# Loading v of an attention unit in two transfers of 128 partitions, one per head

## The chip, the cores and the metric

The kernel runs on one core of a Trainium2 chip. The metric is the device time of one execution in microseconds. The kernel before took 674.45 us, the median of 3 runs (671.71 to 675.39).

A core has a matrix engine (TensorE, PE in the profile, with weight loads shown apart as PEld), three engines for elementwise work (VectorE or DVE, ScalarE or ACT, GpSimd or POOL), and SyncE (SP), which here only issues DMA transfers. Data lie in SBUF, 128 partitions wide; matrix products land in PSUM. Sixteen DMA engines move data between HBM and SBUF.

## The reference

Sparse attention over 8 batches, 8 heads, 576 positions and head dimension 64, then a feed-forward block on the 4608 x 512 result:

```
scores = scale * q @ k.T                   # per batch and head, 576 x 576
mask_local   = (rel >= 0) & (rel < 32)               # heads 0 to 3, rel = pos_i - pos_j
mask_strided = (rel >= 0) & (pos_j % 32 == pos_i % 32)   # heads 4 to 7
attn = softmax(where(mask, scores, -1e9));  out = attn @ v
x = out as (4608, 512)
h = maximum(maximum(x @ w1, x @ w2), x @ w3)         # 512 -> 768
result = h @ w_out                                   # 768 -> 512
```

All values are float32.

## The kernel before, in words

**Units.** Attention is cut into 32 units, four to a batch: two of strided heads, then two of local heads, each unit with two heads (`units`, L234). Units 0 and 1 are strided, 2 and 3 local, and so on. A unit goes through the steps S (scores, on TensorE), X (mask and maximum, DVE), E (exponentials, ACT), N (normalising and a transpose, DVE), V (the product with v, `values`, L426), H and L (the result split in a high and a low part, ACT and DVE).

**How v lies.** On the host, v is laid out in HBM per unit. A strided unit has 128 rows (32 of them used, and in batch 0 only 18), two heads, and 32 groups of 64 values. A local unit has 64 rows (a window of 64 keys), two heads and 18 blocks of 64 values. In SBUF, a unit's v is spread over the 128 partitions in four quarters j of 32 partitions: a quarter holds 8 groups (strided) or 5 blocks and the one before them (local). `load_v` (L256) loads it in one transfer for each quarter, both heads together: four for a strided unit (L280), of 128 KB, or 72 KB in batch 0; for a local unit three of 96 KB (L269), one of 48 KB for the shorter last quarter (L271), and one of 16 KB (L273) for the second half of the last window, which goes to partitions 96 to 127.

**Feed-forward.** The rows are worked in two parts. The first 1024 rows go through plain products (`ff_in`, L525, and `ff_out`, L555) with each float32 weight split into a high and a low part. The other 3584 rows go in four groups of 896 through seven products for each of nine pairs of weight blocks (L779), from weight sums that the kernel builds itself and keeps in HBM scratch; these are read back by a stream of 256 KB transfers (`load_next`, L668) with nine buffers, eight loaded ahead. Each group ends with the output product (L873). Units 16 to 31 run between the products of the first three groups.

**The opening.** The order of the first 100 us is written out by hand in two strings. `LOADS` orders the loads on SyncE: `q0` is one transfer of unit 0's q or k (288 KB; each unit has two), `v0` one of its v, `w0` a weight block of 512 KB. After it follow the remaining weight blocks (w14 to w17, then six of w_out). `OPENING` orders the steps: An to Dn and Cn convert weight block n (A: `convert_begin`, L164 on ACT, reads the loaded block; K: L173 on ACT; B: L183 and L186 on DVE; D: L196 and C: L205, L206 on ACT and POOL); Fn is the first feed-forward product of weight block n on TensorE (f and g are its halves), and Mn (`ff_max`, L540 to L546) takes its result out of one of the two PSUM banks that these products take turns with. Every engine works off its list in order.

```
A0 S0 X0 A1 K0 E0 B0 B1 A2 K1 ...
... f0 U4 D7 f1 K8 D8
C7 A9 L2 K9 S4 V3 X4 C8 H3 L3 g0 A10 g1 A11 A12 M0 B9 D9 K10 E4 B10 M1 D10 K11 B11 C9 D11 A13 F2 ...
```

So on ACT the step M0 stands behind A12, and on TensorE F2 follows g1.

**After the opening**, v and the q and k of a unit are loaded two units ahead: `values(n)` is followed by the loads of v of unit n + 2, and `scores(n)` by those of q and k. SyncE issues everything in one queue: all loads, the scratch writes and reads, and the output of the first part (L561). Each transfer signals one of eight semaphores, which go round, and waits until the transfer before on its semaphore has landed.

Of the kernel before, what the change touches and what calls it, by code (L numbers as in the profile page):

```python
# [7 lines left out]
F32 = mybir.dt.float32  # L8
# [7 lines left out]
B, H, S, D = 8, 8, 576, 64  # L16
STRIDE = 32
DM, DF, DO = 512, 768, 512
P = 128
# [6 lines left out]
NI = S // STRIDE  # L26
EARLY = B - 1
TQ, TK, NT = STRIDE, 2 * STRIDE, NI
# [3 lines left out]
MB = 5  # L32
MS = STRIDE // 4
PAIRED = 1
# [17 lines left out]


LOADS = """
q0 q0 w0 w1 w2 w3 q1 q1 w4 q2 q2 v0 w5 v0 v0 v0 q3 q3 w6 v1 v1 v1 w7 w8 v1 v2 w9 v2 v2 v2 w10 v2 q4 q4 v3 v3 w11 v3 v3 v3
v4 v4 w12 v4 v4 w13 q5 q5 v5 v5 v5 v5
"""
OPENING = """
A0 S0 X0 A1 K0 E0 B0 B1 A2 K1 K2 D0 D1 C0 N0 S1 A3 K3 C1 B2 B3 A4 X1 D2 D3 B4 S2 E1 C2 N1 A5 K4 D4 C3 V0
# [12 lines left out]
def fused_kernel(ctx, tc, qT, kT, qk_loc, qk_str, v_loc, v_str, m_loc, m_str, w1, w2, w3, w_out, out):  # L72
    nc = tc.nc
# [18 lines left out]
    io_early = early.enter_context(tc.tile_pool(name="io_early", bufs=1, side="right"))  # L92
# [7 lines left out]
    pin = tc.keep_in_program_order  # L100
# [17 lines left out]
    for sign in (1, -1):  # L118
        pin(nc.gpsimd.affine_select(
            out=unit, in_=unit, pattern=[[-sign, P]], base=0, channel_multiplier=sign, compare_op=ALU.is_ge, fill=0.0  # L120
# [18 lines left out]


    sources = [(w, j) for j in range(NJ) for w in range(3)] + [(None, j) for j in range(NJ)]
    raws, begun, weight = [], [], {}

    def load_weights(count):
        for _ in range(count):
            i, j = sources.pop(0)
            raw = (wo if i is None else wt).tile([P, 1024], I32, name=f"w{i}_{j}")
            if i is None:
                pin(nc.sync.dma_start(out=raw, in_=w_out.bitcast(I32)[j * P : (j + 1) * P, :]))
            else:  # L150
                src = (w1, w2, w3)[i].bitcast(I32)[:, j * 2 * P : (j + 1) * 2 * P]
                pin(nc.sync.dma_start(
                    out=raw.rearrange("p (c f) -> p c f", c=NKC), in_=src.rearrange("(c p) f -> p c f", p=P)
                ))
            raws.append((raw, i, j))

    def convert_begin():


        raw, i, j = raws.pop(0)  # L160
        words = raw.rearrange("p (n two) -> p n two", two=2)
        low, high = words[:, :, 0], words[:, :, 1]
        mag = wk.tile([P, 512], F32, name="work")
        pin(nc.scalar.activation(out=mag, in_=high.bitcast(F32), func=AF.Abs))  # L164
        pin(nc.gpsimd.tensor_scalar(out=mag, in0=mag, scalar1=W_MOST, scalar2=W_LEAST, op0=ALU.min, op1=ALU.max))
        lows.append(low)
        begun.append((low, high, mag, i, j))

    lows = []

    def convert_low():
        low = lows.pop(0)
# [62 lines left out]
    loaded, v_of = {}, {}  # L235
# [20 lines left out]
    def load_v(n):  # L256
        if n >= len(units):
            return
        b, p = units[n]
        if n in (2, 3):  # L260
            vt = io_early.tile([P, 2 * (MB + 1) * D], F32, name="v_t", bufs=2)
        else:
            vt = io.tile([P, 2 * MS * D], F32, name="v_t", bufs=2)
        if p < 2:

            v_of[n] = v = vt[:, : 2 * (MB + 1) * D].rearrange("p (h m d) -> p h m d", h=2, m=MB + 1)
            last = 3 * MB
            for j in range(3):
                pin(nc.sync.dma_start(out=v[32 * j : 32 * (j + 1)], in_=v_loc[b, p, :32, :, j * MB : (j + 1) * MB + 1, :]))  # L269
                yield  # L270
            pin(nc.sync.dma_start(out=v[96:, :, : NT - last, :], in_=v_loc[b, p, :32, :, last:, :]))  # L271
            yield
            pin(nc.sync.dma_start(out=v[96:, :, NT - last, :], in_=v_loc[b, p, 32:, :, NT - 1, :]))  # L273
            yield
        else:
            v_of[n] = v = vt.rearrange("p (h m d) -> p h m d", h=2, m=MS)
            for j in range(4):

                rows = NI if b < PAIRED else 32
                pin(nc.sync.dma_start(  # L280
                    out=v[32 * j : 32 * j + rows], in_=v_str[b, p - 2, :rows, :, j * MS : (j + 1) * MS, :]
                ))
                yield

    state = {}
# [124 lines left out]
    def pieces_of(b, p, step):  # L410

        at, end = b * S, (b + 1) * S
        while at < end:
            if at < CH:
                first, after, to = 0, CH, [x[:, p, :] for x in x_chunk(0)]
            elif at < PLAIN:
                first, after, to = CH, PLAIN, [place_of(-1)[:, p, :]]
            else:
                k = (at - PLAIN) // BL
                first = PLAIN + k * BL  # L420
                after, to = first + BL, [place_of(k)[:, p, :]]
            after = min(after, end)
            yield (at - b * S) // step, (after - b * S) // step, [x[:, at - first : after - first] for x in to]
            at = after

    def values(n):  # L426

        b, p = units[n]
        pt = state.pop(n)
        v = v_of.pop(n)  # L430
        loaded.pop(n)
        state[n] = to = []
        if p < 2:


            for m in (0, 2, 4, 1, 3, -1):
                for j in range(4):
                    last = min(MB, NT - j * MB) - 1
                    if m > last or (m < 0 and j == 0):
                        continue  # L440
                    js = slice(32 * j, 32 * (j + 1))
                    width = 64 if 0 <= m < last else 32
                    for h in range(2):
                        pin(nc.tensor.matmul(  # L444
                            o[h * D : (h + 1) * D, j, 32 * max(m, 0) : 32 * max(m, 0) + width],
                            v[js, h, m + 1, :],
                            pt[js, h, m * TK + 32 : m * TK + 32 + width] if m >= 0 else pt[js, h, :32],
                            start=m == 0,
                            stop=m == (-1 if j else 3),
                        ))  # L450
            for a0, a1, xs_to in pieces_of(b, p, 1):

                w, at = 32 * MB, a0
                while at < a1:
                    end = min(a1, (at // w + 1) * w)
                    j = at // w
                    if at % w == 0 and a1 >= at + w:
                        end = a1 // w * w
                        src = o[:, j : end // w, :w]
                    else:  # L460
                        src = o[:, j, at - j * w : end - j * w]
                    part = [x[:, at - a0 : end - a0] for x in xs_to]
                    if len(src.shape) == 3:
                        part = [x.rearrange("p (j q) -> p j q", q=w) for x in part]
                    to.append((src, *part))
                    at = end
            return
        if b >= PAIRED:
            for m in range(MS):
                for j in range(2):  # L470
                    js = slice(64 * j, 64 * (j + 1))
                    for h in range(2):
                        pin(nc.tensor.matmul(  # L473
                            o[h * D : (h + 1) * D, j, : 2 * MS * NI].rearrange("p (r m i) -> p r m i", r=2, m=MS)[:, :, m],
                            v[js, h, m, :],
                            pt[js, h, m * 64 : (m + 1) * 64].rearrange("p (r i) -> p r i", r=2)[:, :, :NI],
                            start=True,
                            stop=True,
                        ))
        for m in range(0 if b >= PAIRED else MS):  # L480
            for j in range(4):
                js = slice(32 * j, 32 * j + NI)
                for h in range(2):
                    pin(nc.tensor.matmul(
                        o[h * D : (h + 1) * D, j, m * NI : (m + 1) * NI],
                        v[js, h, m, :],
                        pt[js, h, m * 32 : m * 32 + NI],
                        start=True,
                        stop=True,
                    ))  # L490
        runs = 2 if b >= PAIRED else 4
        src = o[:, :runs, : 4 // runs * MS * NI].rearrange("p j (m i) -> p i j m", i=NI)
        for a0, a1, xs_to in pieces_of(b, p, STRIDE):
            to.append((src[:, a0:a1], *(x.rearrange("p (i j m) -> p i j m", i=a1 - a0, j=runs) for x in xs_to)))
# [144 lines left out]
    for step in OPENING.split():  # L639
        what, n = step[0], int(step[1:])  # L640
# [14 lines left out]
    def placed(n):  # L655

        values(n)
        list(load_v(n + 2))
        leading(n)
        rest(n)  # L660
# [311 lines left out]
```

## Time and profile before

| | |
|---|---|
| time, median of 3 runs | 674.45 us (671.71 to 675.39) |
| span of the profiled execution | 671.9 us (the page gives no other time of it) |
| TensorE clock granted, mean | 0.989 |
| TensorE busy | 647.1 us, 96% |
| DMA moved | 138.36 MB, mean 206 GB/s |
| v transfers | 64 strided (56 of 128 KB, 8 of 72 KB), 80 local (48 of 96 KB, 16 of 48 KB, 16 of 16 KB) |
| median from issue to landing | L280 (128 KB) 4.2 us, L269 3.3 us, L668 3.5 us |

A row of the waits reads: engine, line, `<-` what it waited for, then the sum in us, how many times, and the longest. A row of a timeline reads: start in us, length in us, engine, line, operation, output `<-` inputs, count, and in brackets the idle time before it and what ended it. Lines are those of the kernel before.

### The profile page before, as it was taken

The page shows a single profiled execution, that of the slowest core. Times are in us where ns is not written, and L with a number is a line of the kernel's source. Part 1 is how long each engine was busy: PE and PEld are TensorE (multiplying, and loading weights), DVE is VectorE, ACT ScalarE, POOL GpSimd, SP SyncE. Part 2 cuts the span into 40 slices and gives each one's busy share as a digit, 9 for nine tenths or more (in the row PEclk, how much of TensorE's full clock was granted, in tenths as well). Part 3 has the DMA queues.
Part 4 walks back from the last instruction along what each step waited for, and adds up shares of the span by engine and source line. Part 5 has one row for each costly group of instructions (what it writes and reads, how often), then busy time and mean ns, then how long its engine had stood idle before and what let it go on. Part 6 is the DMA issues. An engine that isn't in the chain of part 4 may idle for free.

```text
span 671.9 us, 18032 instructions
## 1 busy us (share of the span) xinstructions
PE 647.1 (96%) x7408; PEld 553.5 (82%) x7408; DVE 370.8 (55%) x515; ACT 336.5 (50%) x702; POOL 299.4 (45%) x291
## 2 busy tenths in 40 slices
PE   4689999999999999999999999999999999999997
PEld 3467877777778888888888888888899988999986
DVE  5886964676675666476345665643652563224240
ACT  4777656444264445446355455544444554444441
POOL 8779998599942233240134243004334401444410
PEclk9789999999999999999999999999999999999999
DMA  9999974567699777771377899228767714777411
GB/s 297 265 246 366 296 248 133 178 189 233 188 284 326 251 240 257 259 248 63 114 251 236 243 262 276 87 87 213 233 179 216 206 63 124 214 217 216 123 47 63
DMA packets 89371, 138.36 MB, mean 206 GB/s; under 512 B 10153, under 2 KB 39593, under 8 KB 89289
## 3 DMA queue, kind: packets, MB, share of 16 engines
q1 hardware_dynamic: 85256, 129.86, 63.6%
q10 hardware_dynamic: 4032, 7.34, 2.9%
q8 instruction: 59, 0.97, 0.6%
q14 instruction: 24, 0.19, 0.1%
HBM read 111.21 MB, written 25.95 MB: 204 GB/s over the span
## 4 chain that ended last, share of the span: by engine, by line
PE 80%; POOL 9%; DMA 6%; ACT 1%; DVE 1%; issue 1%; SPq 1%; POOLq 0%; ACTq 0%; DVEq 0%
PE f_ps L779 46%; PE f_ps L873 17%; PE f_ps L525 6%; PE f_ps L555 4%; DMA w<-in_w 4%; POOL work L596 2%; PE o_ps L444 2%; POOL work L612 2%; PE s_ps L318 2%; POOL work L588 2%; PE o_ps L473 1%; PE s_ps L340 1%; DMA out<-work 1%; POOL hl L546 1%; POOL sums_low L596 1%; DMA v_t<-in_v_loc 1%
## 5 line engine op out<-in xcount | busy, mean ns | idle before, releaser
L779 PE MATMUL f_ps<-xc,w_stream 128*128 128x448 f32 x1512 | 317.5, 368 | 0.2 <-ACT snap L826 0.2
L779 PEld LDWEIGHTS f_ps<-xc,w_stream 128*128 128x128 f32 x1512 | 280.5, 188 | 26.5 <-ACT snap L826 2.6
L826 ACT COPY snap<-f_ps 128x448 f32<-128x448 f32 x240 | 127.9, 533 | 165.0 <-PE f_ps L779 162.8
L838 POOL TENSOR_TENSOR snap<-snap 128x448 f32<-128x448 f32 x72 | 89.1, 1243 | 148.3 <-ACT snap L826 115.5
L840 DVE TENSOR_TENSOR h_all<-h_all,snap 128x448 f32<-128x448 f32 x96 | 81.2, 887 | 128.9 <-POOL snap L838 128.9
L838 POOL TENSOR_TENSOR h_all<-snap 128x448 f32<-128x448 f32 x36 | 41.4, 1150 | 169.1 <-ACT snap L826 168.1
L873 PE MATMUL f_ps<-wNone,h_parts 128*128 128x512 f32 x504 | 115.0, 389 | 0.0
L873 PEld LDWEIGHTS f_ps<-wNone,h_parts 128*128 128x128 f32 x504 | 94.6, 188 | 19.5
L525 PE MATMUL f_ps<-xh,w 128*128 128x512 f32 x288 | 95.8, 402 | 0.0
L525 PEld LDWEIGHTS f_ps<-xh,w 128*128 128x128 f32 x288 | 54.7, 190 | 12.7 <-ACT xh L498 0.3
L525 PE MATMUL f_ps<-xl,w 128*128 128x512 f32 x144 | 56.7, 394 | 0.8 <-DVE xl L503 0.8
L864 DVE TENSOR_TENSOR h_parts<-h_all,h_parts 128x768 fp32r<-128x768 f32 (+2 forms) x40 | 27.2, 712 | 30.3 <-ACT h_parts L863 30.1
L879 ACT COPY work<-f_ps 128x512 f32<-128x512 f32 x28 | 16.4, 585 | 46.1 <-PE f_ps L873 46.1
L683 DVE TENSOR_TENSOR xc<-x_block,xc 128x896 fp32r<-128x896 f32 x28 | 29.8, 1086 | 11.1 <-ACT xc L680 11.1
L397 DVE TENSOR_REDUCE s_ps<-s_ps 128x10 f32<-128x640 f32 (+2 forms) x30 | 23.2, 772 | 20.3 <-ACT s_ps L386 20.3
L407 DVE STREAM_TRANSPOSE pt<-s_ps 128x640 f32<-128x640 f32 (+2 forms) x32 | 32.5, 1017 | 1.1
L525 PEld LDWEIGHTS f_ps<-xl,w 128*128 128x128 f32 x144 | 27.4, 190 | 6.2 <-DVE xl L503 1.1
L555 PE MATMUL f_ps<-wNone,hh 128*128 128x512 f32 x96 | 30.6, 400 | 0.3 <-issue 0.3
L863 ACT CAST h_parts<-h_all 128x768 fp32r<-128x768 f32 (+2 forms) x40 | 24.5, 642 | 12.0 <-DVE h_all L840 5.4
L386 ACT ACTIVATE s_ps<-s_ps 128x640 f32<-128x640 f32 (+2 forms) x30 | 19.5, 651 | 21.9 <-DVE s_ps L370 21.9
L340 PEld LDWEIGHTS s_ps<-qk_t 64*32 64x32 f32 x1408 | 16.5, 116 | 15.2 <-DMA qk_t<-in_qT 7.0
L680 ACT CAST xc<-x_block 128x896 fp32r<-128x896 f32 x28 | 25.8, 947 | 3.4 <-DVE xc L683 1.2
(87 smaller groups left out, 681.6 us busy)
## 6 DMA issues: line engine op xcount, KB each, us to landing
w_stream<-scratch SPq DMA_DIRECT2D x252, 256.0 KB, 3.5
w<-in_w SPq DMA_DIRECT2D x18, 512.0 KB
qk_t<-in_qT SPq DMA_DIRECT2D x28, 288.0 KB, 3.8
qk_t<-in_kT SPq DMA_DIRECT2D x28, 288.0 KB, 5.9
v_t<-in_v_str SPq DMA_DIRECT2D x56, 128.0 KB, 4.2
out<-work ACTq DMA_DIRECT2D x28, 256.0 KB, 2.0
scratch<-w SPq DMA_DIRECT2D x27, 256.0 KB, 3.3
v_t<-in_v_loc SPq DMA_DIRECT2D x48, 96.0 KB, 3.3
```

The lines of the kernel that those rows point to most:

```text
L407: pin(nc.vector.transpose(pt[:, :, : nm * at], s_ps[:, :, : nm * at]))
L525: pin(nc.tensor.matmul(f_ps, w[:, kc, :], x[:, kc, :], start=(kc == 2 and n == 0), stop=(kc == 1 and n == 2)))
L555: pin(nc.tensor.matmul(f_ps, h[:, ts], w, start=(j == 0 and n == 0), stop=(j == NJ - 1 and n == 2)))
L680: pin(nc.scalar.copy(out=x[m][:, 0], in_=src))
L683: pin(nc.vector.tensor_tensor(out=x[m][:, 1], in0=src, in1=x[m][:, 0].bitcast(F32), op=ALU.subtract))
L779: pin(nc.tensor.matmul(out_, w[:, wl, fs], x[:, xl, k, :], start=start and k == 0 and n == 0, stop=k == 1 and n == 2, skip_group_check=not ...
L826: pin(nc.scalar.copy(out=t, in_=src))
L838: pin(nc.gpsimd.tensor_tensor(out=h if i == 0 else u, in0=u, in1=t, op=ALU.add))
L840: pin(nc.vector.tensor_tensor(out=h, in0=h, in1=u, op=ALU.max))
L863: pin(nc.scalar.copy(out=to[:, 0, j0:j1], in_=src))
L864: pin(nc.vector.tensor_tensor(out=to[:, 1, j0:j1], in0=src, in1=to[:, 0, j0:j1].bitcast(F32), op=ALU.subtract))
L873: pin(nc.tensor.matmul(outs[t], h, w, start=(j == 0 and n == 0), stop=(j == NJ - 1 and n == 2)))
```

## The change

`load_v` now issues one transfer per head. For a strided unit it fills all 128 partitions with 2 KB each; the source address pattern walks the four quarters outermost, then 32 rows, then 8 groups of 64 values. Batch 0 is no longer an exception: all 32 rows are loaded. For a local unit a hand-made address pattern does the same with quarters that overlap by one block (6 blocks, 1.5 KB a partition); the last quarter reads on past its third block into the following addresses, which no product uses. The small third transfer goes to a place of its own behind the two heads (`last`), and `values` reads it there. The early pool's v tile grows by two blocks of 64 values. `LOADS` has fewer v entries, and in part another order. The edit in `convert_begin` only makes the two halves of a weight block when it is loaded.

```diff
-q0 q0 w0 w1 w2 w3 q1 q1 w4 q2 q2 v0 w5 v0 v0 v0 q3 q3 w6 v1 v1 v1 w7 w8 v1 v2 w9 v2 v2 v2 w10 v2 q4 q4 v3 v3 w11 v3 v3 v3
-v4 v4 w12 v4 v4 w13 q5 q5 v5 v5 v5 v5
+q0 q0 w0 w1 w2 w3 q1 q1 w4 q2 q2 v0 w5 v0 q3 q3 w6 v1 v1 w7 w8 v2 w9 v2 v2 w10 q4 q4 v3 v3 w11 v3 v4 v4 w12 w13 q5 q5 v5 v5
...
         if n in (2, 3):
-            vt = io_early.tile([P, 2 * (MB + 1) * D], F32, name="v_t", bufs=2)
+            vt = io_early.tile([P, (2 * (MB + 1) + 2) * D], F32, name="v_t", bufs=2)
...
-            v_of[n] = v = vt[:, : 2 * (MB + 1) * D].rearrange("p (h m d) -> p h m d", h=2, m=MB + 1)
-            last = 3 * MB
-            for j in range(3):
-                pin(nc.sync.dma_start(out=v[32 * j : 32 * (j + 1)], in_=v_loc[b, p, :32, :, j * MB : (j + 1) * MB + 1, :]))
+            v = vt[:, : 2 * (MB + 1) * D].rearrange("p (h m d) -> p h m d", h=2, m=MB + 1)
+            last = vt[:, 2 * (MB + 1) * D : (2 * (MB + 1) + 2) * D].rearrange("p (h d) -> p h d", h=2)
+            v_of[n] = v, last
+            for h in range(2):
+                rows = v_loc[b, p, :32, h].rearrange("r m d -> r (m d)")
+                runs = bass.AP(tensor=rows.tensor, offset=rows.offset, ap=[[MB * D, 4], rows.ap[0], [1, (MB + 1) * D]])
+                pin(nc.sync.dma_start(out=v[:, h].rearrange("p m d -> p (m d)"), in_=runs))
                 yield
-            pin(nc.sync.dma_start(out=v[96:, :, : NT - last, :], in_=v_loc[b, p, :32, :, last:, :]))
+            pin(nc.sync.dma_start(out=last[96:], in_=v_loc[b, p, 32:, :, NT - 1, :]))
             yield
-            pin(nc.sync.dma_start(out=v[96:, :, NT - last, :], in_=v_loc[b, p, 32:, :, NT - 1, :]))
-            yield
         else:
             v_of[n] = v = vt.rearrange("p (h m d) -> p h m d", h=2, m=MS)
-            for j in range(4):
-
-                rows = NI if b < PAIRED else 32
-                pin(nc.sync.dma_start(
-                    out=v[32 * j : 32 * j + rows], in_=v_str[b, p - 2, :rows, :, j * MS : (j + 1) * MS, :]
-                ))
+            for h in range(2):
+                src = v_str[b, p - 2, :32, h].rearrange("r (j m) d -> j r (m d)", m=MS)
+                pin(nc.sync.dma_start(out=vt[:, h * MS * D : (h + 1) * MS * D], in_=src))
                 yield
...
-                            v[js, h, m + 1, :],
+                            last_v[js, h] if j == 3 and m == last else v[js, h, m + 1, :],
```

On SyncE, the stretch of the opening in which units 1 and 2 are loaded (`w_2` and `w_3` are the weight blocks w6 to w10), before:

```order
L152 DMA w_2_194<-in_w 128x4x256
L280 DMA v_t<-in_v_str 18x2x512 x3
L152 DMA w_2_200<-in_w 128x4x256
L152 DMA w_2_202<-in_w 128x4x256
L280 DMA v_t<-in_v_str 18x2x512
L269 DMA v_t<-in_v_loc 32x2x384
L152 DMA w_3_207<-in_w 128x4x256
L269 DMA v_t<-in_v_loc 32x2x384 x2
L271 DMA v_t<-in_v_loc 32x2x192
L152 DMA w_3_212<-in_w 128x4x256
L273 DMA v_t<-in_v_loc 32x2x64
```

and now:

```order
L152 DMA w_2_192<-in_w 128x4x256
L277 DMA v_t<-in_v_str 128x1x512 x2
L152 DMA w_2_197<-in_w 128x4x256
L152 DMA w_2_199<-in_w 128x4x256
L269 DMA v_t<-in_v_loc 128x1x384
L152 DMA w_3_203<-in_w 128x4x256
L269 DMA v_t<-in_v_loc 128x1x384
L271 DMA v_t<-in_v_loc 32x2x64
L152 DMA w_3_207<-in_w 128x4x256
```

The whole of v1 now stands ahead of w7 and w8, and the whole of v2 ahead of w10.

On SyncE, the stretch with v3 to v5 and w11 to w14 (`w_3_221` or `w_3_215` is w11, `w_4` w12 to w14), before:

```order
L269 DMA v_t<-in_v_loc 32x2x384 x2
L152 DMA w_3_221<-in_w 128x4x256
L269 DMA v_t<-in_v_loc 32x2x384
L271 DMA v_t<-in_v_loc 32x2x192
L273 DMA v_t<-in_v_loc 32x2x64
L280 DMA v_t<-in_v_str 32x2x512 x2
L152 DMA w_4_229<-in_w 128x4x256
L280 DMA v_t<-in_v_str 32x2x512 x2
L152 DMA w_4_233<-in_w 128x4x256
L246 DMA qk_t<-in_qT 128x576
L246 DMA qk_t<-in_kT 128x576
L280 DMA v_t<-in_v_str 32x2x512 x4
```

and now:

```order
L269 DMA v_t<-in_v_loc 128x1x384 x2
L152 DMA w_3_215<-in_w 128x4x256
L271 DMA v_t<-in_v_loc 32x2x64
L277 DMA v_t<-in_v_str 128x1x512 x2
L152 DMA w_4_221<-in_w 128x4x256
L152 DMA w_4_223<-in_w 128x4x256
L243 DMA qk_t<-in_qT 128x576
L243 DMA qk_t<-in_kT 128x576
L277 DMA v_t<-in_v_str 128x1x512 x2
```

The whole of v4 now stands ahead of w12, of which half stood behind it. On the other engines the order of instructions is the same.

More of the change, by code (lines that the diff above doesn't have):

```diff
@@ L141, in fused_kernel @@
     sources = [(w, j) for j in range(NJ) for w in range(3)] + [(None, j) for j in range(NJ)]
-    raws, begun, weight = [], [], {}
+    raws, begun, lows, weight = [], [], [], {}
     def load_weights(count):
@@ L154, in load_weights @@
                 ))
-            raws.append((raw, i, j))
+            low, high = (raw.rearrange("p (n two) -> p n two", two=2)[:, :, x] for x in range(2))
+            raws.append((low, high, i, j))
+            lows.append(low)
     def convert_begin():
-        raw, i, j = raws.pop(0)
-        words = raw.rearrange("p (n two) -> p n two", two=2)
-        low, high = words[:, :, 0], words[:, :, 1]
+        low, high, i, j = raws.pop(0)
         mag = wk.tile([P, 512], F32, name="work")
@@ L165, in convert_begin @@
         pin(nc.gpsimd.tensor_scalar(out=mag, in0=mag, scalar1=W_MOST, scalar2=W_LEAST, op0=ALU.min, op1=ALU.max))
-        lows.append(low)
         begun.append((low, high, mag, i, j))
-    lows = []
     def convert_low():
@@ L433, in values @@
         if p < 2:
+            v, last_v = v
             for m in (0, 2, 4, 1, 3, -1):
```

## The prediction

> **What bounds the kernel now.** I read the page first, then the busy time by stage, then who waits for DMAs in the opening. From the page, the span, the engines and the queue that SyncE issues on (packets, MB, share of 16 DMA engines):
>
> ```profile
> span 671.9 us, 18032 instructions
> PE 647.1 (96%) x7408; PEld 553.5 (82%) x7408; DVE 370.8 (55%) x515; ACT 336.5 (50%) x702; POOL 299.4 (45%) x291
> q1 hardware_dynamic: 85256, 129.86, 63.6%
> ```
>
> By stage; after a stretch's length stand the busy times of PE, PEld, DVE, ACT and POOL, and the last three figures are TensorE's clock, the DMA engines' share and GB/s:
>
> ```profile
> 0.00:46.00 46.00, 27.94 (x923) 21.58 (x924) 32.92 (x58) 28.92 (x71) 35.61 (x56) 0.85 0.95 272
> 46.00:67.00 21.00, 20.20 (x205) 16.33 (x204) 15.39 (x24) 15.21 (x29) 21.00 (x22) 1.00 1.07 341
> 207.00:299.00 92.00, 92.00 (x1269) 80.96 (x1268) 54.23 (x79) 45.91 (x103) 30.64 (x26) 1.00 0.80 261
> ```
>
> From 46 us on TensorE is busy almost throughout, 92.00 of 92.00 us in the stage that streams weights. There is little to win there, and lateness that reaches TensorE is lost for good, because nothing behind it can catch up. In the first 46 us it idles for 18 us while the DMA engines are at 0.95: the opening is bound by arrivals. The waits there:
>
> ```profile
> PE o_ps L484 <- DMA v_t<-in_v_str: 2.7, 3, 2.0
> PE o_ps L444 <- DMA v_t<-in_v_loc: 1.0, 1, 1.0
> ACT work L164 <- DMA w<-in_w: 8.2, 5, 4.6
> SPq L668 <- PE f_ps L779: 205.7, 165, 26.7
> ```
>
> So at most 3.7 us can come directly from v arriving sooner. ACT's weight conversions wait longer for their loads than TensorE does for v, and every v load stands in one queue ahead of some of them.
>
> **The change, part by part.** *Fewer issues.* A strided unit issues 2 transfers for 4, a local one 3 for 5. The issues of L280, of 18 partitions and of 32 (ns, min/median/max):
>
> ```profile
> L280 SPq DMA_DIRECT2D v_t<-in_v_str x8: 758/782/1024, 9.0 to 23.1; - x8
> ...
> L280 SPq DMA_DIRECT2D v_t<-in_v_str x56: 560/592/1274, 37.6 to 411.3; - x56
> DMA to landing us min/median/max: 3.6/4.2/8.6
> ```
>
> Thirty-two units save 2 issues each, 64 x 0.59 = 38 us of SyncE. Nobody gains by it: in the stream it is SyncE that waits, 205.7 us at L668 for TensorE to free a buffer. I count 0.
>
> *More bytes, another order.* A strided unit of batch 0 grows from 288 to 512 KB (32 rows for 18), a local unit from 352 to 400 (the last quarter reads past its end): 544 KB for units 0 to 3, 2.0 us of the opening at 272 GB/s. Against it, v1 comes ahead of w7 and w8 as a whole, and v2 ahead of w10. With an even spread these about cancel.
>
> *How the bytes spread over the DMA engines.* This term decides. Before, the outermost loop of a v load's source counts 32 rows times two heads (36 in batch 0). Now it counts four quarters: `"r (j m) d -> j r (m d)"` and the hand-made pattern that begins with `[MB * D, 4]` both have a 4 outermost, against 128 partitions at the other end. No view prints the engines of a transfer, but the trace's semaphore records count its landings: 574 transfers leave 9,128, sixteen each (eight records are missing), except that each 18-partition one leaves ten, one of them right after the issue and nine spread over the landing. The rows above show the same eight as odd: 0.78 us to issue against 0.59. Nine is the largest number up to 16 that divides both 18 and 36; by that arithmetic 4 and 128 give four. The ends are thus 16 engines, as all other transfers have, and four. I take four, since the one odd shape in the trace follows the arithmetic, and the same four each time, so that the load piles up on them.
>
> The Trainium skill, "DMA: Bandwidth & Descriptors", section "Why a DMA increments its semaphore by 16 and not by 1", states this rule, the largest number up to 16 that divides the slowest dimension of both patterns, and that the lowest-numbered engines serve; the nine landings agree, and no run here yet shows a four. Against it the same page, section "Rules for kernel authors", asks to coalesce many small transfers into a large one, which speaks for this change; by that alone the time would be the first rival's.
>
> *Price of four engines.* One engine carries 261 / (16 x 0.80) = 20.4 GB/s in the stream, 272 / (16 x 0.95) = 17.9 in the crowded opening. The fastest slice of 207 to 299 us:
>
> ```profile
> GB/s 354 289 322 346 369 173 281 136 267 296 320 238 236 98 225 319 363 255 239 217 383 299 143 302 156 195 338 357 180 305 159 91 345 348 289 262 126 132 312 371
> ```
>
> 383 / 16 = 23.9. A strided v puts 512 / 4 = 128 KB on each of the four, 6.4 us at 20.4; a local one 97 KB, 4.9 us. They carry their sixteenth of all else too: 18 KB of each q or k, 32 KB of each w. Summed in the queue's new order from 2.5 us, they are done with v0 at 24.0 us (428 KB), v1 at 33.8 (624), v2 at 43.5 (817), v3 at 53.4 (1014) and w12 at 61.4 (1174 KB, 1.20 MB). When units 0 to 3 use v now (TensorE's timeline):
>
> ```profile
> 20.41 0.29 PE L484 MATMUL o_ps<-pt,v_t 18*64 18x18 f32 x4 [0.46 <-DMA v_t<-in_v_str]
> 29.87 1.90 PE L484 MATMUL o_ps<-pt,v_t 18*64 18x18 f32 x116 [1.95 <-DMA v_t<-in_v_str]
> 35.19 0.73 PE L444 MATMUL o_ps<-pt,v_t 32*64 32x32 f32 x31 [0.98 <-DMA v_t<-in_v_loc]
> 42.04 1.14 PE L444 MATMUL o_ps<-pt,v_t 32*64 32x64 f32 x84
> ```
>
> The lateness grows, 4, 4, 8, 11 us. Then, from the chain of waits and ACT's timeline:
>
> ```profile
> 45.24 13.05 PE f_ps L525 x56
> ```
>
> ```profile
> 45.77 0.68 ACT L164 ACTIVATE work<-w 128x512 f32<-128x512 f32 x1 [0.61 <-POOL w L206]
> 46.36 0.57 ACT L540 COPY h_max<-f_ps 128x512 f32<-128x512 f32 x1
> ...
> 56.30 0.66 ACT L164 ACTIVATE work<-w 128x512 f32<-128x512 f32 x1
> ```
>
> At 45.77 stands step A12, which reads w12; behind it on ACT waits M0, which frees the PSUM bank that F2 writes. F2 follows eight matmuls into the run of 56, at 45.24 + 8 x 13.05 / 56 = 47.1. With w12 at 61.4, M0 ends at 61.4 + 0.68 + 0.57 = 62.6: TensorE is 15.5 us late, the lateness of v3 contained in it. Behind w12, w13, q5, v5 and w14 bring 228 KB, 11.4 us, to 73; their reader A14 (56.30) would by then run at 72, which adds 1. Bounds: at 17.9 GB/s w12 comes at 69.7 and F2 24 us late, at 23.9 at 52.8 and 7. I take **+15**, since four engines beside twelve idle ones should run nearer to 20.4. The same sum for the kernel now, 720 KB at 17.9, gives 43.7, against a reader that starts at 45.77.
>
> *Middle.* SyncE's queue, and the chain of waits:
>
> ```profile
> 113.61 3.16 SPq L280 DMA_DIRECT2D v_t<-in_v_str  x4
> 117.98 0.85 SPq L561 DMA_DIRECT2D out<-work  x2
> ```
>
> ```profile
> 117.98 4.42 DMA out<-work
> ...
> 123.09 3.04 DMA out<-work
> 126.29 1.28 POOL work L588
> ...
> 191.86 1.66 PE o_ps L444 x70
> ```
>
> The store hands a work buffer on to POOL, whose sums then run nearly without a gap to 189 us and release TensorE at 191.86. v9 is issued ahead of it: 2.3 us to start and 6.4 on four engines end at 122.3, q and k 1.8 and the store 0.8 at 124.9 for 122.4. **+2**; bounds 0 (POOL makes it up) and 5.
>
> *Start of the stream.*
>
> ```profile
> 197.90 0.97 SPq L668 DMA_DIRECT2D w_stream<-scratch  x2
> 198.97 2.48 SPq L280 DMA_DIRECT2D v_t<-in_v_str  x4
> 202.12 0.97 SPq L668 DMA_DIRECT2D w_stream<-scratch  x2
> ```
>
> v17 stands between the first weight loads: 6.4 us on four engines, after v16's 6.4. The third product, due at about 210, would wait. **+2**; bounds 0 and 6.
>
> *Stream.* Nine products and a unit take 244.32 - 231.01 = 13.31 us:
>
> ```profile
> 221.09 9.92 PE f_ps L779 x48
> 231.01 0.90 PE s_ps L340 x61
> ...
> 244.32 0.90 PE s_ps L340 x61
> ```
>
> ```profile
> L668 SPq DMA_DIRECT2D w_stream<-scratch x252: 319/320/1585, 197.9 to 628.5; - x126
> ...
> DMA to landing us min/median/max: 2.8/3.5/5.9
> ```
>
> In that time the four engines must move 9 x 16 + 36 + 128 = 308 KB (315 kB): 13.2 us at 23.9, 15.5 at 20.4; with a local unit 277 KB, 11.9 or 13.9. A burst of 6.4 on top of 3.5 to landing just fits the eight products, 9.92 us, that are loaded ahead. I count 0; the other end is 12.
>
> Sum: 15 + 2 + 2 = 19 us on the profiled span of 671.9, 691. The page gives no other time of that execution; the runs' median of 674.45 is 2.55 above the span, so 693.
>
> **Rivals.**
> - *All 16 engines: not slower.* Place: the opening. The idle 1.95 and 0.98 us at L484 and L444 go; 22 KB more per engine ahead of w12 are 1.2 us later weights, half of which M0's wait passes on: 674.45 - 2.9 + 0.6 = 672. For it: every transfer of 128 partitions leaves sixteen landings. Against it: none of them has an outermost loop under 16. It decides if the busiest engine's work ahead of w12 grows by under 50 KB (454 with four).
> - *Four engines, and the stream starves.* At 20.4 a strided unit lacks 2.2 us, a local one 0.6; over six units 8.4, of which the loads ahead absorb half: 4 in each of three groups, 705. Against it: slices of 383 GB/s.
> - *Four engines, but the opening swallows most.* At 23.9 F2 is 7 us late, and middle and start cost nothing: 681. Against it: no slice of the opening holds that rate.
>
> **How the numbers follow.** Forecast, 687 to 700: 55%. Starving stream, 700 to 715: 19%. Light opening, 676 to 687: 14%. All 16: 12%. The range 677 to 711 leaves out the last and the top of the second. Under 0.5%, 3.4 us, cannot be told from no change here. Slower: 55 + 19 + 14 less 1 = 87%; the last case splits into 7% faster and 5% same, and same takes the 1.
>
> **What would show it.** Four landings to a v transfer; L164's wait for w grows past 15 us, and TensorE's unbroken run of L525 begins near 61; the DMA share of the first 60 us falls well below 0.95, since twelve engines idle; w_stream's landing goes from 3.5 towards 7 us with no wait at L779. Wrong if the share stays, or if TensorE is under 5 us late at 100 us; the stream's term is wrong if its nine products take over 13.6 us.

## The result, and the profile after

The changed kernel takes 713.38 us, the median of 6 runs (709.80 to 716.91), against 675.28 (671.71 to 676.30) for the kernel before, run beside it: a ratio of 1.0574, with a 95% interval from 1.0543 to 1.0606. It is slower, as forecast, but by 38 us where 18 were forecast, and 2.4 us above the range.

From the page of the changed kernel, the span, the engines and SyncE's queue:

```profile
span 713.9 us, 17959 instructions
...
PE 658.4 (92%) x7408; PEld 560.7 (79%) x7408; DVE 370.4 (52%) x515; ACT 337.5 (47%) x702; POOL 300.0 (42%) x291
...
q1 hardware_dynamic: 83744, 131.10, 61.0%
```

TensorE issues the same 7,408 matmuls. It is busy for 11.3 us more than before (647.1) and idle for 30.7 more. The queue carries 1.24 MB more, and its packets take a smaller share of sixteen engines (61.0% for 63.6%), so the loss isn't one of total traffic. The spans differ by 42.0 us, more than the medians, since this execution of the changed kernel is one of its longer ones (715.68 us); the account by stage below is made on the spans.

Busy times by stage, the changed kernel (columns as in the prediction; the stages begin and end at the same matmuls as those of the kernel before, below):

```profile
0.00:46.00 46.00, 21.77 (x761) 17.13 (x762) 26.59 (x48) 24.17 (x61) 29.82 (x50) 1.00 0.78 236
46.00:67.00 21.00, 14.56 (x187) 10.86 (x187) 12.93 (x21) 10.31 (x20) 13.48 (x14) 0.84 0.70 193
...
114.10:228.70 114.60, 108.19 (x1591) 85.70 (x1583) 70.36 (x98) 51.80 (x129) 82.09 (x80) 0.97 0.58 190
...
228.70:328.34 99.64, 95.39 (x1276) 83.61 (x1275) 55.54 (x80) 46.73 (x104) 31.83 (x27) 0.98 0.82 247
328.34:460.66 132.32, 122.15 (x1378) 105.81 (x1377) 69.89 (x95) 62.35 (x131) 32.98 (x28) 0.99 0.68 193
460.66:576.23 115.57, 115.57 (x1009) 102.05 (x1009) 52.39 (x68) 54.41 (x102) 32.00 (x27) 0.98 0.58 171
```

and the kernel before:

```profile
99.60:206.20 106.60, 104.87 (x1590) 83.69 (x1583) 70.33 (x98) 51.51 (x129) 81.92 (x80) 1.00 0.65 202
...
206.20:299.74 93.54, 93.54 (x1276) 82.39 (x1275) 54.97 (x80) 46.64 (x104) 31.27 (x27) 1.00 0.80 263
299.74:420.49 120.75, 120.58 (x1377) 105.02 (x1377) 68.57 (x94) 62.20 (x131) 32.75 (x28) 1.00 0.68 207
420.49:534.21 113.72, 113.72 (x1009) 100.73 (x1009) 55.19 (x70) 54.32 (x102) 32.68 (x28) 1.00 0.59 174
```

In the first 46 us TensorE issues 761 matmuls where it issued 923, while the DMA engines' share falls from 0.95 to 0.78: fewer bytes arrive, and some of the engines have nothing to do. The clock of 1.00 in the first row is not a measurement: the trace has no clock record before 47.82 us, and single matmuls of 128x512 take 0.63 us from 44 us on and 0.40 behind 48. Put together from the ends of these stages and from F2, which begins at 60.8 after and at 47.1 before:

| stage | before, us | after, us | more |
|---|---|---|---|
| start to F2 | 47.1 | 60.8 | 13.7 |
| F2 to the first outputs of chunk 0 | 52.5 | 53.3 | 0.8 |
| middle, to the first streamed product | 106.6 | 114.6 | 8.0 |
| stream, group 0 | 93.5 | 99.6 | 6.1 |
| stream, group 1 | 120.8 | 132.3 | 11.6 |
| group 2 and the rest | 251.4 | 253.2 | 1.8 |

One execution of a kernel differs from the next by some microseconds (671.71 to 676.30 for the kernel before), so a single stage is good to about 2 us.

Who waits, in the changed kernel (engine, line and tile waited for, us in total, times, longest; its lines stand 5 lower than those of the kernel before, so L774 is L779 and L520 is L525):

```profile
ACT work L164 <- DMA w<-in_w: 16.7, 8, 5.5
...
PE f_ps L774 <- DMA w_stream<-scratch: 14.2, 9, 3.6
PE o_ps L439 <- DMA v_t<-in_v_loc: 11.4, 6, 3.3
...
PE o_ps L479 <- DMA v_t<-in_v_str: 6.4, 3, 3.0
...
PE f_ps L520 <- ACT h_max L535: 4.8, 1, 4.8
```

TensorE waited 3.7 us for v before, and 17.8 now. The 14.2 us for streamed weights and the 4.8 for ACT's h_max are new: there was no such row. These five rows are the four-engine theory at work in each stage: v itself late, and the weights queued behind v late as well.

*The opening*, in the chain of waits of the changed kernel:

```profile
46.28 13.28 DMA w<-in_w
...
59.64 0.66 ACT work L164
60.30 0.48 ACT h_max L535
...
60.82 13.08 PE f_ps L520 x48
```

This is the path that the prediction named: w12, then A12 and M0 on ACT, then F2. The trace's semaphore records of w12 show why it takes 13.28 us: its first landing comes at 51.17 and its last at 59.56, though the transfer runs on all sixteen engines. Twelve have landed by 51.56, and the other four follow from 59.03 on, 8 us behind: as many engines as a v transfer uses.

*The middle*, in TensorE's timeline of the changed kernel (idle time before a row and its cause in brackets):

```profile
139.52 0.50 PE L520 MATMUL f_ps<-xh,w 128*128 128x512 f32 x1 [1.44 <-ACT work L555]
...
206.23 1.18 PE L439 MATMUL o_ps<-pt,v_t 32*64 32x64 f32 x82 [2.17 <-DMA v_t<-in_v_loc]
...
214.90 1.15 PE L439 MATMUL o_ps<-pt,v_t 32*64 32x64 f32 x82 [1.30 <-DMA v_t<-in_v_loc]
...
234.65 9.26 PE L774 MATMUL f_ps<-xc,w_stream 128*128 128x448 f32 x36 [2.09 <-DMA w_stream<-scratch]
```

The first is the output store behind v9, which takes 8.21 us to land (4.42 before). The next two are v of the two local units that are loaded last ahead of the stream, and the last is the third product of the stream.

*The stream*, in the chain of waits of the changed kernel, one unit of group 0 and the end of group 1:

```profile
274.11 0.57 SPq L277
...
274.73 0.53 SPq L277
...
275.30 10.61 DMA w_stream<-scratch
...
286.04 1.45 PE f_ps L774 x6
```

```profile
446.23 11.71 DMA w_stream<-scratch
...
458.08 2.58 PE f_ps L774 x6
460.66 30.33 PE f_ps L868 x126
```

In the stream a weight block that is issued right behind a strided v is 10.6 to 11.8 us under way, for 3.5 in the median of the kernel before. In the second fence the stall is followed by slow work: six matmuls take 2.58 us for 1.45, and the 126 behind them 30.33 (28.57 before). The clock in the stretches around it:

```profile
456.00:458.00 2.00, 0.00 (x0) 0.00 (x0) 1.56 (x2) 0.00 (x0) 0.54 (x1) 0.86 0.51 191
458.00:462.00 4.00, 3.92 (x10) 3.44 (x11) 0.74 (x2) 1.13 (x3) 0.00 (x0) 0.50 0.62 192
462.00:470.00 8.00, 8.00 (x32) 6.46 (x32) 1.49 (x4) 1.53 (x4) 0.00 (x0) 0.86 0.08 30
```

The granted clock is 0.50 just after the stall and 0.86 on average over the next 8 us; the clock records have one half up to 464.25 us and full speed from there. So this wait of 3.58 us costs about 2.9 more in slow matmuls (1.1 in the six, 1.8 in the 126).

### The profile page after: what moved, and what is told of

The parts are those of the page before. It is cut to its first block, busy times and chain, and to the rows that moved or that the text cites. A ratio compares the mean times of both kernels' runs of the same rounds, so it can differ in the third digit from the quotient of the medians.

```text
span 713.9 us, 17959 instructions
## 1 busy us (share of the span) xinstructions
PE 658.4 (92%) x7408; PEld 560.7 (79%) x7408; DVE 370.4 (52%) x515; ACT 337.5 (47%) x702; POOL 300.0 (42%) x291
## 4 chain that ended last, share of the span: by engine, by line
PE 62%; DMA 24%; POOL 6%; SPq 5%; issue 1%; ACT 1%; DVE 1%; ACTq 0%; POOLq 0%
PE f_ps L774 32%; PE f_ps L868 16%; DMA w_stream<-scratch 13%; PE f_ps L520 6%; DMA v_t<-in_v_loc 5%; PE f_ps L550 3%; DMA w<-in_w 2%; DMA qk_t<-in_kT 2%; PE o_ps L468 2%; SPq L277 1%; PE o_ps L439 1%; POOL work L591 1%; DMA out<-work 1%; PE s_ps L335 1%; SPq L152 1%; POOL work L607 1%
## 5 line engine op out<-in xcount | busy, mean ns | idle before, releaser
L774 PE MATMUL f_ps<-xc,w_stream 128*128 128x448 f32 x1512 | 320.5, 370 | 14.4 <-DMA w_stream<-scratch 14.2
L774 PEld LDWEIGHTS f_ps<-xc,w_stream 128*128 128x128 f32 x1512 | 282.3, 189 | 42.1 <-issue 15.8
L868 PE MATMUL f_ps<-wNone,h_parts 128*128 128x512 f32 x504 | 116.8, 393 | 0.0
L868 PEld LDWEIGHTS f_ps<-wNone,h_parts 128*128 128x128 f32 x504 | 96.1, 191 | 20.1
L520 PE MATMUL f_ps<-xh,w 128*128 128x512 f32 x288 | 99.0, 414 | 6.3 <-ACT h_max L535 4.8
L520 PEld LDWEIGHTS f_ps<-xh,w 128*128 128x128 f32 x288 | 56.7, 197 | 20.0 <-ACT h_max L535 5.3
L520 PE MATMUL f_ps<-xl,w 128*128 128x512 f32 x144 | 58.3, 405 | 0.4 <-DVE xl L498 0.4
L678 DVE TENSOR_TENSOR xc<-x_block,xc 128x896 fp32r<-128x896 f32 x28 | 29.8, 1087 | 15.6 <-ACT xc L675 15.6
L520 PEld LDWEIGHTS f_ps<-xl,w 128*128 128x128 f32 x144 | 28.4, 197 | 6.3 <-DVE xl L498 0.7
L439 PEld LDWEIGHTS o_ps<-pt,v_t 32*64 32x64 f32 x1344 | 17.7, 136 | 16.8 <-DMA v_t<-in_v_loc 8.4
L439 PE MATMUL o_ps<-pt,v_t 32*64 32x64 f32 (+1 forms) x1344 | 20.0, 231 | 11.4 <-DMA v_t<-in_v_loc 11.4
```

What stands on the lines that cost most here:

```text
L439: pin(nc.tensor.matmul(o[h * D : (h + 1) * D, j, 32 * max(m, 0) : 32 * max(m, 0) + width], last_v[js, h] if j == 3 and m == last else v[js ...
L520: pin(nc.tensor.matmul(f_ps, w[:, kc, :], x[:, kc, :], start=(kc == 2 and n == 0), stop=(kc == 1 and n == 2)))
L678: pin(nc.vector.tensor_tensor(out=x[m][:, 1], in0=src, in1=x[m][:, 0].bitcast(F32), op=ALU.subtract))
L774: pin(nc.tensor.matmul(out_, w[:, wl, fs], x[:, xl, k, :], start=start and k == 0 and n == 0, stop=k == 1 and n == 2, skip_group_check=not ...
L868: pin(nc.tensor.matmul(outs[t], h, w, start=(j == 0 and n == 0), stop=(j == NJ - 1 and n == 2)))
```

## The experiments

Three questions: is it the number of DMA engines, and not the size or the shape of the transfers; how the loss divides over the stages; and what in the stream turns late bytes into stalls. In the expectations C is the theory that the distance by which weights are loaded ahead is too short for a v that fills four engines; D, that the eight transfers in flight are the limit. The kernel before took 676.07 us beside the runs with sixteen and eight engines, further ahead and with the heads apart, 677.22 beside the three that divide the loss, and 675.12 beside the last two. Where not said otherwise the edits are to the changed kernel.

### Sixteen engines, same transfers

The inputs v_loc and v_str are laid out on the host as the 128 rows that a head's transfer writes, so that both sides of it have 128 outermost (a local unit's small third reads an array of its own, in place of an input that no line uses). Two transfers per unit, their size and the order of the queue stay; the kernel computes the same.

```diff
-                src = v_str[b, p - 2, :32, h].rearrange("r (j m) d -> j r (m d)", m=MS)
-                pin(nc.sync.dma_start(out=vt[:, h * MS * D : (h + 1) * MS * D], in_=src))
+                pin(nc.sync.dma_start(out=vt[:, h * MS * D : (h + 1) * MS * D], in_=v_str[b, p - 2, h]))
...
+    v_str = v_str[:, :, :32].reshape(B, 2, 32, 2, 4, MS, D).transpose(0, 1, 3, 4, 2, 5, 6).reshape(B, 2, 2, P, MS * D)
```

> The changed kernel, with v laid out on the host so that the source of each per-head transfer is 128 rows in one loop (two transfers of 128 partitions per unit, the same bytes to the same places, the same order of loads). Theory A (the four engines that an outermost loop of four allows): all of the loss goes, 671 to 676 us, since the busiest engine has 742 KB ahead of w12 instead of 1174; a transfer leaves sixteen landings and w12's reader starts near 46 us. Rival B (larger transfers, the new order of loads, more bytes, whatever the spread): stays above 700 us.

676.52 us; ratio to the kernel before 1.0008 (0.9992 to 1.0024). The whole loss is gone, with two transfers per unit and their bytes kept. The semaphore records of a v transfer now count sixteen; in the changed kernel they count five, one of them right after the issue and four at the landing. From the busy times by stage:

```profile
0.00:46.00 46.00, 25.18 (x858) 19.30 (x858) 30.51 (x53) 26.26 (x65) 32.55 (x53) 0.78 1.01 337
```

The DMA engines are full in the opening and move 337 GB/s (236 in the changed kernel). No wait of TensorE for v or for w_stream is left. The new layout also makes the source of a transfer one piece of HBM, which this run by itself doesn't separate from the number of engines. The next run keeps the layout, apart from one spare row per group, and still pays for fewer engines; and of w12's sixteen landings in the changed kernel it is four that are late. So the price was that of the four engines. Four engines with the new layout were not run.

### Eight engines

The same host layout, in eight groups of 16 rows with one unused row behind each, so that the groups stay apart as a dimension and the outermost loop counts 8.

```diff
+SPREAD = 8
...
+                pin(nc.sync.dma_start(
+                    out=vt[:, h * MS * D : (h + 1) * MS * D], in_=v_str[b, p - 2, h, :, : P // SPREAD]
+                ))
```

> As the run with 128 rows, but the source is eight groups of 16 rows with a row of padding between groups, so that the outermost loop counts eight. Theory A: eight engines, nine or ten landing records a transfer less seven; 885 KB ahead of w12 on the busiest engine, w12 read about 2 us later than before the change; a pair of v takes 3.4 us of an engine in the stream, which the weights loaded ahead cover: 675 to 681 us. Rival (the loss grows in proportion to the bytes on the busiest engine, a third of the way from 16 engines to four): 687 to 690 us. Rival B: above 700 us.

680.39 us; 1.0064 (1.0039 to 1.0089). The records count nine, one right after the issue and eight at the landing. From the chain of waits, the opening's path:

```profile
39.00 12.03 DMA w<-in_w
...
51.11 0.66 ACT work L165
51.78 0.48 ACT h_max L535
...
52.30 11.17 PE f_ps L520 x48
```

The path is the same, F2 5 us late for 14 with four engines, and there is no wait for w_stream at all. Sixteen, eight and four engines thus cost 0, 4 and 38 us: twice the engines take away nine tenths of the loss, because in the stream eight engines stay within what the weights loaded ahead cover.

The Trainium skill, page "DMA: Bandwidth & Descriptors", section "Why a DMA increments its semaphore by 16 and not by 1", has a transfer run on the largest number up to 16 that divides the slowest dimension of both patterns. The records of five, nine and sixteen (one more than four and eight where the issuing engine adds the rest itself) agree with it in all three kernels.

### The loss divided over the units

The new loads for some units only, the old ones for the others (the order of the opening's loads is then the old one where its units are old):

```diff
+HEADS = lambda n: n < 6
...
+            if not HEADS(n):
+                for j in range(4):
+                    rows = NI if b < PAIRED else 32
+                    pin(nc.sync.dma_start(
+                        out=v[32 * j : 32 * j + rows], in_=v_str[b, p - 2, :rows, :, j * MS : (j + 1) * MS, :]
+                    ))
+                    yield
+                return
```

New for units 0 to 5, loaded in the opening (`n < 6`):

> The changed kernel's loads for units 0 to 5 alone (the order of loads of the change too); all later units load v by quarters as before. Theory A as the two traces have it: TensorE is 14.5 us late from the opening on and nothing is added or given back later: 688 to 691 us. Rival F (part of the later lateness is a consequence of the opening's, through POOL's sums or the queue of SyncE): 694 or more. Rival G (later stages give some of it back): under 686.

New for units 18 to 31, loaded while weights are streamed (`n >= 18`):

> Before's loads for units 0 to 17, the changed loads for units 18 to 31, that is for those that are loaded while the weights are streamed. From the traces the stream lost 17 to 19 us, with what stood in it from the start: theory A with C, 688 to 693 us. If the stream only suffers because it starts with the backlog of v16 and v17, 680 us or less.

New for units 6 to 31 (`n >= 6`):

> Before's loads for units 0 to 5, the changed loads for all from unit 6 on: middle and stream without the opening. If the three stages add up, 675 + 8 + 19 = 700 to 705 us, and with the run of the opening alone (about 690) this makes the 38 us of the change. If the middle's 8 us come only because the opening made everything late, 691 to 696.

As expected, the opening alone costs 13.4 us (690.59; 1.0194, 1.0171 to 1.0216), the stream alone 12.3 (689.49; 1.0178, 1.0152 to 1.0203), and everything behind the opening 21.1 (698.34; 1.0328, 1.0283 to 1.0374), so that the middle with the start of the stream has 21.1 - 12.3 = 8.8. The 698.34 us lie between the two expectations, 700 to 705 if the stages add up and 691 to 696 if the middle's loss came from the opening alone. Opening and later units together make 34.5 of the 38.1; the rest, 3.6, appears only when both are there and isn't explained. The traces point to the middle, which is 5.3 us longer than before with `n >= 6`, not longer with `n < 6`, and 8.0 longer in the changed kernel. In the kernel with `n >= 18`, who waits (lines 19 higher than in the changed kernel):

```profile
PE f_ps L793 <- DMA w_stream<-scratch: 10.5, 7, 2.7
```

Its loads up to the stream are those of the kernel before. In the kernel with `n < 6` TensorE has no wait for w_stream. So the stream's stalls come from its own units and aren't an echo of the late opening.

### Loaded further ahead

Ten streamed weight blocks ahead in place of eight. To make room the buffers of `snap`, which TensorE's products pass through, go from 8 to 6.

```diff
-AHEAD = 8
+AHEAD = 10
...
-            for name, bufs in (("xc", 1), ("wst", AHEAD + 1), ("snap", 8), ("hsp", 3)):
+            for name, bufs in (("xc", 1), ("wst", AHEAD + 1), ("snap", 6), ("hsp", 3)):
...
+    for _ in range(AHEAD - 8):
+        load_next()
     supers()
```

> The changed kernel with two more weight buffers in the stream (ten loaded ahead for eight; six buffers for copies out of PSUM instead of eight make the room). Theory C (the stream stalls because weights issued behind a pair of v land 10.6 to 10.9 us later and only eight products, 9.9 us, are loaded ahead): TensorE's waits for w_stream fall from 14.2 us to under 4, the time falls by 10 to 16 us, to 698 to 704. Rival D (the eight transfers in flight: SyncE waits 60 us in the stream for v to land before it may issue the next weights): nothing gained, within 3 us of the changed kernel, 711 to 716.

699.87 us; 1.0353 (1.0326 to 1.0380), 13.5 us less than the changed kernel. Its waits for streamed weights:

```profile
PE f_ps L774 <- DMA w_stream<-scratch: 1.4, 1, 1.4
```

Nine waits of 14.2 us have become one of 1.4. Two blocks more, 2.5 us of TensorE's work, cover nearly all of it; the bytes, the four engines and the number of transfers in flight are unchanged. That is C, and D falls. The one that is left stands at 434.9 us, behind a block that is 13.06 us under way.

### The two heads apart

In the stream the second head's transfer (and a local unit's third) is issued five products after the first.

```diff
+    late_v = []
...
-        list(load_v(n + 2))
+        to_come = load_v(n + 2)
+        if n < 16:
+            list(to_come)
+        else:
+            next(to_come, None)
+            late_v.append(to_come)
...
+            if k % 9 == 5 and late_v:
+                list(late_v.pop())
```

> The changed kernel; in the stream the second head's transfer of a unit's v (and the small third) is issued five products after the first. Theory C (the burst of two transfers on four engines is what the weights queue behind): weights wait behind one transfer at a time, about 3.6 us less, within what is loaded ahead; TensorE's waits for w_stream fall under 4 us and the time by 12 to 18 us, to 696 to 702. Rival E (the four engines have more to carry in 13.3 us than they can, 308 KB at 18 to 19 GB/s being 17 us, burst or not): within 3 us of the changed kernel.

706.54 us; 1.0457 (1.0426 to 1.0488). Its waits:

```profile
PE f_ps L781 <- DMA w_stream<-scratch: 7.8, 6, 2.1
```

About half of the wait goes, and 6.8 us of the time. That is neither what was expected by C, waits under 4 us and 696 to 702 us, nor by the rival E, no gain. Half a burst at a time still leaves the same bytes on four engines, but each block behind it is held for less long. The direction is that of C, the size isn't.

### Why does the sixteen-engine kernel win nothing?

With sixteen engines, w12 lands at 39.7 us (44.96 in the kernel before) and the last load of the opening at 57.7 (66.8), with fewer issues, and still the time is that of the kernel before. F2 begins at 50.9 us, later than the 47.1 before, though w12's reader was expected near 46. A repeat gave 676.12 us, 1.0012 (0.9998 to 1.0026), with F2 at 49.3. From TensorE's timeline, the first run and then the repeat:

```profile
27.53 1.33 PE L332 MATMUL s_ps<-qk_t 64*32 64x64 f32 x68 [1.92 <-issue]
...
34.19 1.26 PE L476 MATMUL o_ps<-pt,v_t 18*64 18x18 f32 x69 [4.32 <-issue]
```

```profile
27.94 1.33 PE L332 MATMUL s_ps<-qk_t 64*32 64x64 f32 x68 [2.61 <-issue]
...
32.69 1.26 PE L476 MATMUL o_ps<-pt,v_t 18*64 18x18 f32 x69 [2.40 <-issue]
```

TensorE stops twice, in the middle of a run of equal matmuls, and "issue" says that the profile shows nothing that it waits for. ACT in turn waits for the matmuls behind the second stop, 5.42 us in the first run. Theory H: it waits for its own instructions. The page of the first run has a queue for them:

```profile
q8 instruction: 59, 0.97, 0.6%
```

These are 59 transfers of 16 KB, for 14,816 matmuls and weight loads, and two of them stand at 25.03 and 31.63 us in the trace, amid 350 to 370 GB/s of loads and ahead of the two stops' ends.

To test it, the loads from w9 on are issued only when ACT has done the exponentials of unit 2. ACT copies one column to `flag`, and SyncE stores that to scratch, which holds the queue until then; the store is extra, nothing is left out. The edit is to the sixteen-engine kernel.

```diff
+        if step == "G2":
+            pin(nc.scalar.copy(out=flag, in_=state[2][6][:, 0, :1]))
+            pin(nc.sync.dma_start(out=mark, in_=flag))
+            load(all_loads[now:])
+            load_weights(len(sources))
```

> The run with 128 rows, with one addition: the loads from w9 on are issued only after ACT has done the exponentials of unit 2 (a copy of one column marks it, and SyncE stores that column to scratch). In the run with 128 rows the opening's loads were all down by 57.7 us instead of 66.8, yet nothing was won: TensorE sat for 1.9 and 4.3 us near 27 and 34 us with nothing to wait for in the profile, while the DMA engines were at 1.07 to 1.09. Theory H (TensorE then waits for its own code: 59 transfers of 16 KB on the instruction queue for 14,816 instructions, which share the saturated DMA engines): with the engines idle for some us the gap near 34 us shrinks below 1.5 us, F2 starts 2 to 4 us sooner than its 50.9, and the time is 671 to 674. Rival I (the gap has another cause, or the later loads cost what the gap gives): no gain, 675 to 681.

> The run with 128 rows once more, beside the paced one: within 0.3% of the kernel before, F2 at 50 to 52 us, and if the gaps near 27 and 34 us belong to the kernel and not to one execution, they stand there again with 4 us or more together.

679.84 us; 1.0074 (1.0050 to 1.0097): slower, as the rival I had it, and F2 begins at 56.3 us, later instead of sooner. Two rows of its timeline and two of its stages:

```profile
31.29 1.25 PE L476 MATMUL o_ps<-pt,v_t 18*64 18x18 f32 x69 [1.02 <-issue]
...
41.63 1.24 PE L436 MATMUL o_ps<-pt,v_t 32*64 32x64 f32 x57 [7.09 <-DMA v_t<-in_v_loc]
```

```profile
25.00:30.00 5.00, 3.46 (x132) 2.19 (x133) 3.47 (x5) 4.71 (x22) 3.31 (x5) 0.50 0.22 69
30.00:35.00 5.00, 1.99 (x90) 1.59 (x81) 4.56 (x10) 3.11 (x8) 3.37 (x4) 0.50 0.86 27
```

With loads at 69 GB/s around it, the second stop is 1.02 us for 4.32 and 2.40. That agrees with H, but the first stop is still 1.54 us long (1.92 and 2.61 in the others), though hardly any load was moving then (54 GB/s from 26 to 27 us, 24 in the next), and the loads that were held back then cost more: TensorE waits 7.09 us for v. The stretch from 30 to 35 us is odd. The marker, 512 bytes in 128 pieces of 4, was issued at 29.09 and landed at 37.78, while the engines' share is 0.86 at only 27 GB/s; the loads behind it were late with it. So the run can't tell how much the stops by themselves cost, and H stays open. No version ran faster than the kernel before.

## Why the prediction was right or wrong

- **How the bytes spread, right.** Four landings to each v transfer, five records with the one right after the issue. The share of the DMA engines in the first 46 us is 0.78, and L164's wait for w is 16.7 us, past the 15 that were named.
- **Price of four engines, right.** Predicted were v1 at 33.8, v2 at 43.5, v3 at 53.4 and w12 at 61.4 us, F2 at 62.6 and +15 with A14; the semaphore records have v1 at 33.4, v2 at 42.4, v3 at 51.4 and w12 at 59.6, F2 began at 60.8, and the two rows of the table make 14.5. The opening by itself costs 13.4 us in the run with `n < 6`.
- **Fewer issues and more bytes, right.** With sixteen engines the same issues and bytes cost nothing that can be measured (1.0008), though they don't earn anything either.
- **Middle, mis-sized: +2 with bounds of 0 and 5, measured 8.0.** The store behind v9 was the place that was named, and it stalls TensorE for 1.44 us, by way of ACT, whose next output waits for the buffer. Left out were the two local units ahead of the stream: their v, issued at 197.66 and 203.69 us, is 8.5 and 11.2 us under way (4.7 and 5.7 for the same two units before) and costs 3.75 us of idle time. Of the 8.0 us, 4.7 are more idle time (6.41 less 1.73 in the windows) and 3.3 the same work at a lower clock.
- **Start of the stream, right in place and wait.** The third product waits 2.09 us for the predicted 2. The slower clock behind it adds 1.8 (36 matmuls in 9.26 us; at 9.92 for 48 they take 7.44).
- **Stream, the step that failed: "A burst of 6.4 on top of 3.5 to landing just fits the eight products, 9.92 us".** The sum had no margin, and two parts of it were short. In the unit at 274 us v starts moving some 3.5 us after its issue, as counted, since the q, k and weights ahead are still landing until 277.7. Its two transfers then take 7.6 us (the second alone 3.66 us for 64 KB on each engine, 17.9 GB/s), not 6.4. The weight block behind lands another 0.6 later, which the sum didn't have. That is 11.8 us from the issue of v, for 11.0 of work that is loaded ahead (eight products and the scores between them). From 230 us on the second transfer of a unit moved at 14 to 23 GB/s per engine, 18.6 in the median, so that 20.4 was a little high, and the fastest slice, 23.9, which was held against the starving stream, says nothing about four engines. Measured: 14.2 us in nine waits and, with the clock, 19.5 us over the three groups, of which the start is 3.9; the term that was counted as 0, with 12 as its other end, came to 15.6. The prediction's own test, nine products in over 13.6 us, shows it: 286.04 to 300.79 are 14.8. Of the 23 us by which the measured 42.0 exceed the sum of 19, this term makes 15.6, the middle 6.0 and the start 1.9, less 0.5 of the opening.
- **The rival "four engines, and the stream starves"** named this and put it at 4 us in each of three groups, 705 us. It had the mechanism, but the groups got 6.1 (with the start), 11.6 and 1.8. It stood too low by the middle, 6 us, and by the slow clock.
- **A price that no term had: the clock.** From 47.82 us on, five of the seven stalls over 1.4 us bring on half the clock, for 3.41 or 6.83 us. TensorE is busy for 20.5 us in these stretches, so that about 10 us are lost in them, an estimate at half speed; its busy time has grown by 11.3 us for the same matmuls.
- **"All 16 engines: not slower"** was wrong for this change. With sixteen engines the kernel is indeed not slower, but the gain of 2.4 us that this rival had doesn't come: 676.5 us, beside 676.1 for the kernel before.

## What to carry to other kernels

Before transfers are merged, count the outermost loop of both sides: here a source rearranged to "4 quarters x 32 rows" put everything on four engines although 128 partitions are written, and 128 rows in one loop cost nothing. A transfer on a few engines delays all that is queued behind it on those engines, so its price is read at the next loads' readers, and in a stream it must fit into the work loaded ahead with the time of the block behind it counted too. Where a stall can't be avoided, add the slow clock behind it to its price.

## What the runs showed of the hardware

- **The clock after a stall.** The stall of 1.44 us at 139.5 is followed by 4 us at a clock of 0.57 (row below), and the one of 3.58 us by 4 us at 0.50 and 8 at 0.86; yet behind a stall of 2.66 us, at 441.6, six matmuls took 1.45 us, the normal time. So length alone doesn't decide. The trace's clock records show an even step: the five stretches of half clock begin at 58.06, 139.98, 208.25, 235.56 and 457.42 us, all a multiple of 3.41 us apart, and last one or two such steps. In the step ahead of each, TensorE had been busy for 1.35, 1.80, 2.02, 1.33 and 0.49 us. The stall of 2.66 us lies across the border of two steps, with 2.03 and 2.14 us of work in them. But the step from 423.29, with 1.84 us of work, was not followed by half clock, so this share alone doesn't decide either. The Trainium skill, page "TensorE: Matmul & The Clock Gate", section "Part 1: The HAM clock gate", describes half clock until a window of about 3.4 us has been busy, with windows that run freely; 0.57 over 4 us is 3.4 us at one half, and the even step agrees with windows that run freely. What a window needs to count as busy is not shown by any run here.

From the busy times by stage of the changed kernel, the 4 us behind the stall of 1.44 us, and the steps ahead of it and behind it:

```profile
139.50:143.50 4.00, 3.98 (x10) 3.12 (x11) 0.96 (x2) 2.14 (x4) 3.05 (x3) 0.57 0.71 236
...
136.57:139.98 3.41, 1.80 (x67) 1.47 (x67) 2.04 (x4) 1.07 (x2) 0.38 (x1) 1.00 0.20 74
...
139.98:143.40 3.42, 3.42 (x10) 2.63 (x9) 0.52 (x1) 1.68 (x3) 2.58 (x3) 0.50 0.80 266
```

- **Instructions under full DMA load.** TensorE's unexplained stops of 1.9 to 4.3 us with 350 to 370 GB/s of loads under way, and of 1.54 and 1.02 with the loads held back; the cause stays open.
- **A store of 128 pieces of 4 bytes** took 8.7 us to land, in the one run that has it.
